# A new order of all five instruction queues in a fused linear-attention and GEGLU block

## The chip, the core and the metric

The kernel runs on one core of a Trainium2 chip. The time is device microseconds of one execution; the figure for a kernel is the median of its runs. A profiled execution, taken by the hardware profiler, stands beside the runs and has a time of its own. The engines are called as in the profile: PE is TensorE, DVE is VectorE, ACT is ScalarE, POOL is GpSimd and SP is SyncE, which here only issues DMAs. POOL issues the stores and some other DMAs.

## The reference

The input x has 2048 rows of 1024 values in bf16. The work is a block with two residual branches, both conditioned by a vector c:

```python
mod = (_silu(c) @ w_mod).reshape(1, 6, 1, -1)
sa, ca, ga, sb, cb, gb = (mod[:, i] for i in range(6))
h = layernorm(x) * (1 + ca) + sa
x = x + ga * A(h, wqkv, wo)          # linear attention, 32 heads of 32
h = layernorm(x) * (1 + cb) + sb
x = x + gb * ((gelu(h @ w_gate) * (h @ w_up)) @ w_down)   # inner width 3584
```

A takes phi(t) = (t + 1 where t > 0, else exp(t)) + 1e-6 of q and k, forms kv = sum of phi(k) v and z = sum of phi(k) per head, and returns (phi(q) kv) / (phi(q) z + 1e-6), multiplied by wo.

## The kernel before, in words

**The work.** Matrix products are done in float16 by schemes of seven products in place of eight, in part nested once more. They need sums and differences of blocks of the operands and of the results; most of these are `tt_op` (L786) on VectorE, and copies out of PSUM on ScalarE (L1092). The rows are handled in two halves of 1024, g = 0 and g = 1. In the profiled execution of before the stages lie about so:

| stage | us from the span's start |
|---|---|
| start: first rows normed, conditioning vector, first weights | 0 to 30 |
| `kvq_phase`: products for k, v and q | 30 to 156 |
| `merge_phase` and `wo_phase`: attention output, first residual, second norm of half 0 | 156 to 240 |
| `gate_up(0)`: gate and up products of half 0 | 240 to 409 |
| `down_out(0)`: down product of half 0 | 409 to 478 |
| `gate_up(1)` | 478 to 650 |
| `down_out(1)` | 650 to 732 |

The places in the code that the prediction speaks of:

- `late_norm(1)` (L1484 to L1503) norms the eight tiles (128 rows each) of half 1 while `gate_up(0)` runs. A tile is loaded into one of three buffers (`x2e_ring`), its statistics are taken on ScalarE (L1494, L1495), completed on VectorE (L1496, L1498) and POOL (L1497, a `pow`), the normed tile is written on ScalarE into one of three buffers (`xhe_ring`, L1499), and POOL stores it to DRAM (L1500). Tiles 0, 3 and 6 use the same buffer of the ring.
- `h2_load` (L1471 to L1474) brings the stored tiles back turned, by a transposing DMA on SP's queue (L1473); `h2_mod` then scales and shifts them. `rows_turned` (L1049) is the same for the first norm.
- `down_out(g)` begins with the differences A1x = A21 − A22 and A11 − A21, in seven steps c of two tiles each (L1921, L1922). A1x lies at 144 KB of a partition, and both rings of `late_norm` lie there too (`x2e_ring` at 144 KB, `xhe_ring` at 150 KB, 2 KB for each buffer), so c = 0 to 2 write over `x2e_ring`, and c = 3, 4, 5 over the three buffers of `xhe_ring`.
- In `down_out`, `nested` (loads L1991, products L2001, 256 wide) and `plain` (loads L1948, products L1952, 512 wide) are the seven products; "b11", "b21", "t0", "t1" and so on name the one. A load goes into memory that an earlier product's weights held.
- In `gate_up`, the products are L1723 (512 wide) and L1734 (256 wide).

**What sets the order.** Nothing is issued as the code is run. Each operation is recorded in a `Plan` with its engine, its predecessors (by memory) and a modelled cost. `Plan.order` then makes a list schedule: it sweeps forward and back over the operations with the modelled costs and due times, keeps the best of 32 forward sweeps, and hands it to `refine`. `refine` moves each engine's operations by a table written into the file: word i of `SHIFTS[engine]` says how many places away the operation stands that is to come at place i ("z13" is thirteen places that keep theirs):

```python
seqs[e] = [seqs[e][i + d] for i, d in enumerate(shifts)]
```

So the table alone decides the final order of each queue. TensorE has 4515 recorded operations, VectorE 1425, ScalarE 815, POOL 191 and SP 233. An engine takes its queue strictly in that order and waits at each operation for the semaphores of its predecessors.

Of the kernel before, what the change touches and what calls it, by code (L numbers as in the profile page):

```python
# [21 lines left out]
        "z13 8 8 8 8 z4 -8 -8 -8 -8 z20 16 16 16 16 -4 -4 -4 -4 -4 -4 -4 -4 -4 -4 -4 -4 -4 -4 -4 -4 4 4 4 4 -4 -4 -4 "  # L22
        "-4 16 16 16 16 -4 -4 -4 -4 -4 -4 -4 -4 z4 4 4 4 4 -12 -12 -12 -12 20 20 20 20 -4 -4 -4 -4 -4 -4 -4 -4 -4 -4 "
        "-4 -4 -4 -4 -4 -4 8 8 8 8 8 8 8 8 8 8 8 8 8 8 8 8 -12 -12 -12 -12 4 4 4 4 4 4 4 4 16 16 16 16 -36 -36 -36 -36 "
        "4 4 4 4 -4 -4 -4 -4 -12 -12 -12 -12 4 4 4 4 -4 -4 -4 -4 4 4 4 4 4 4 4 4 4 4 4 4 4 4 4 4 12 12 12 12 4 4 4 4 "
        "-4 -4 -4 -4 -28 -28 -28 -28 32 32 32 32 32 32 32 32 z8 -16 -16 -16 -16 -16 -16 -16 -16 16 16 16 16 16 16 16 "
        "16 -16 -16 -16 -16 -16 -16 -16 -16 -16 -16 -16 -16 -16 -16 -16 -16 16 16 16 16 16 16 16 16 -8 -8 -8 -8 -8 -8 "
        "-8 -8 -8 -8 -8 -8 -8 -8 -8 -8 z8 16 16 16 16 16 16 16 16 16 16 16 16 -12 -12 -12 -12 -12 -12 -12 -12 -12 -12 "
        "-12 -12 -12 -12 -12 -12 8 8 8 8 8 8 8 8 20 20 20 20 20 20 20 20 28 28 28 28 28 28 28 28 -24 -24 -24 -24 33 33 "
        "33 33 33 33 33 33 -20 -20 -20 -20 -20 -20 -20 -20 -20 -20 -20 -20 -44 -44 -44 -44 34 34 34 34 34 34 34 34 -24 "  # L30
        "-24 -24 -24 -24 -24 -24 -24 -11 -11 -11 -11 -3 -21 -21 -21 -21 -21 32 32 32 32 32 32 32 32 -4 -4 -4 -4 -12 "
        "-12 -12 -12 24 24 24 24 24 24 24 24 -32 -32 -32 -32 -32 -32 -32 -32 -16 -16 -16 -16 -12 -12 -12 -12 -20 -20 "
        "-20 -20 -16 -16 -16 -16 4 4 4 4 40 40 40 40 -8 -8 -8 -8 28 28 28 28 4 4 4 4 36 36 36 36 z4 32 32 32 32 -24 "
        "-24 -24 -24 -24 -24 -24 -24 -24 -24 -24 -24 36 36 36 36 36 36 36 36 -24 -24 -24 -24 -8 -8 -8 -8 -8 -8 -8 -8 "
        "-32 -32 -32 -32 -32 -32 -32 -32 4 4 4 4 -8 -8 -8 -8 -16 -16 -16 -16 32 32 32 32 4 4 4 4 4 4 4 4 -24 -24 -24 "
        "-24 -12 -12 -12 -12 8 8 8 8 24 24 24 24 12 12 12 12 -16 -16 -16 -16 z4 -16 -16 -16 -16 z4 -28 -28 -28 -28 4 4 "
        "4 4 -4 -4 -4 -4 4 4 4 4 -4 -4 -4 -4 4 4 4 4 -4 -4 -4 -4 4 4 4 4 -4 -4 -4 -4 4 4 4 4 -4 -4 -4 -4 z8 36 36 36 "
        "36 z4 4 4 4 4 4 4 4 4 -8 -8 -8 -8 -20 -20 -20 -20 16 16 16 16 -8 -8 -8 -8 -8 -8 -8 -8 -8 -8 -8 -8 -8 -8 -8 -8 "
        "z20 8 8 8 8 -4 -4 -4 -4 -4 -4 -4 -4 24 24 24 24 16 16 16 16 8 8 8 8 z4 -16 -16 -16 -16 -16 -16 -16 -16 -16 "
        "-16 -16 -16 4 4 4 4 -4 -4 -4 -4 4 4 4 4 12 12 12 12 12 12 12 12 -12 -12 -12 -12 -4 -4 -4 -4 16 16 16 16 8 8 8 "  # L40
        "8 -4 -4 -4 -4 8 8 8 8 8 8 8 8 -12 -12 -12 -12 -36 -36 -36 -36 4 4 4 4 -4 -4 -4 -4 z4 64 75 -2 -2 -2 -2 2 2 2 "
        "2 -6 -6 -6 -6 30 62 62 62 62 62 62 62 -6 -6 -6 -6 19 19 19 19 19 19 19 19 19 19 19 -13 -13 -13 -13 -21 -21 "
        "-21 -21 -33 -33 -33 -33 -21 -21 -21 -21 12 12 12 12 12 12 12 12 12 12 -31 -31 -31 -31 8 32 32 32 32 32 32 32 "
        "32 8 8 8 8 8 8 8 8 32 32 32 32 32 32 32 32 32 32 32 32 32 32 32 32 -64 -64 -64 -64 -64 -64 -64 -64 -48 -48 "
        "-48 -48 -56 -56 -56 -56 -20 -20 -20 -20 28 28 28 28 -32 -32 -32 -32 -16 -16 -16 -16 20 -25 -25 -25 -25 3 3 3 "
        "3 -5 -5 -5 -5 8 16 16 16 16 16 16 16 16 16 16 16 16 16 16 16 16 -18 -18 -18 -18 -34 -34 -34 -34 -16 -16 -16 "
        "-16 -16 -16 -16 -16 8 8 -2 -2 -2 -2 -2 -2 -2 -2 4 4 4 4 4 14 12 -7 -7 -7 -7 -1 -1 -1 -1 -6 -2 -2 -2 -2 18 18 "
        "2 2 2 2 -6 -6 -6 -6 4 4 4 4 -4 -4 -4 -4 2 2 2 2 -13 -15 14 5 5 5 5 -5 -5 -5 -5 6 -6 -1 -1 -1 -1 -10 10 10 10 "
        "10 z6 4 4 4 4 -14 -14 -14 -14 z13 35 35 35 35 35 35 35 35 11 11 11 11 11 11 11 11 11 11 11 11 11 11 11 11 27 "
        "27 27 27 27 27 27 27 11 11 11 11 11 11 11 11 -40 -40 -40 -40 -40 -40 -40 -40 -40 -40 -40 -40 -40 -40 -40 -40 "  # L50
        "-40 -40 -40 z8 64 64 64 64 4 4 4 4 4 4 4 4 -12 -12 -12 -12 -12 -12 -12 -12 -4 -4 -4 -4 -4 -4 -4 -4 -4 -4 -4 "
        "-4 -4 -4 -4 -4 -4 -4 -4 -4 -4 -4 -4 -4 -4 -4 -4 -4 -4 -4 -4 -4 -4 -4 -4 -4 -4 -4 -4 -4 -4 -4 -4 -4 -4 -4 -4 "
        "-4 8 8 8 8 8 8 8 8 -8 -8 -8 -8 -8 -8 -8 -8 z8 12 12 12 12 4 4 4 4 -8 -8 -8 -8 -8 -8 -8 -8 z12 20 20 20 20 -4 "
        "-4 -4 -4 16 16 16 16 -8 -8 -8 -8 -8 -8 -8 -8 16 16 16 16 16 16 16 16 -16 -16 -16 -16 -16 -16 -16 -16 16 16 16 "
        "16 4 4 4 4 12 12 12 12 -20 -20 -20 -20 -4 -4 -4 -4 -24 -24 -24 -24 4 4 4 4 -4 -4 -4 -4 2 2 2 2 10 10 10 10 -8 "
        "-3 -3 -3 -3 5 5 5 5 5 5 5 5 -20 -12 -12 -12 -12 4 4 4 4 -4 -4 -4 -4 4 4 4 4 8 8 8 8 12 12 12 12 -12 -12 -12 "
        "-12 -8 -8 -8 -8 12 12 12 12 -8 -8 -8 -8 -4 -4 -4 -4 10 10 6 6 24 24 24 24 -12 -12 -12 -12 -8 -8 -8 -8 4 4 -2 "
        "-2 -2 -2 -10 -10 -10 -10 6 6 6 6 12 12 -6 -6 4 4 4 4 6 6 -18 -18 -18 -18 -8 -8 10 10 10 10 -4 -4 -4 -4 -4 -4 "
        "-4 -4 10 10 10 10 34 34 34 34 -12 -12 -6 -6 -6 -6 6 6 2 2 -16 -16 -6 -6 -6 -6 28 28 4 4 26 26 -8 -8 -8 -8 14 "
        "14 14 14 -30 -30 -4 -4 z4 20 20 20 20 -18 -18 -18 -18 -8 -8 -30 -30 -30 -30 -4 -4 -4 -4 -4 -4 -4 -4 38 38 38 "  # L60
        "38 -8 -8 4 4 4 4 -6 -6 -6 -6 z4 2 2 -2 -2 -20 -20 -16 -16 -4 -4 -4 -4 z2 4 4 -2 -2 -2 -2 14 14 14 14 z4 -20 "
        "-20 -20 -20 -4 -4 -4 -4 -4 -4 50 50 50 50 -4 -4 -4 -4 2 2 2 2 10 10 10 10 -12 -12 -12 -12 10 10 10 10 -16 -16 "
        "40 40 -14 -14 34 34 -16 -16 -16 -16 -10 -10 -10 -10 8 8 z2 -10 -10 -10 -10 -10 -10 -10 -10 8 8 8 8 2 2 -38 "
        "-38 16 16 -8 -8 -8 -8 16 16 z4 -28 -28 -28 -28 -4 -4 -4 -4 -2 -2 -2 -2 6 6 6 6 30 30 30 30 2 2 2 2 4 4 z2 -16 "
        "-16 -16 -16 28 28 28 28 -2 -2 -2 -2 4 4 -26 -26 -6 -6 -16 -16 -16 -16 6 6 6 6 z2 -6 -6 -6 -6 4 4 4 4 -24 -24 "
        "-24 -24 18 18 18 18 -4 -4 -4 -4 -4 -4 18 18 14 14 32 32 32 32 -12 -12 -12 -12 -10 -10 -10 -10 -4 -4 -4 -4 30 "
        "30 -22 -22 -18 -18 2 2 24 24 4 4 -12 -12 -12 -12 4 4 4 4 4 4 4 4 4 4 -16 -16 -16 -16 8 8 8 8 8 8 -2 -2 -2 -2 "
        "-36 -36 -36 -36 12 12 12 12 z2 -6 -6 -6 -6 -4 -4 -4 -4 26 26 4 4 -8 -8 2 2 20 20 z4 10 10 -14 -14 -14 -14 -2 "
        "-2 18 18 18 18 -12 -12 -12 -12 4 4 -12 -12 -12 -12 z4 4 4 4 4 4 4 4 4 18 18 -20 -20 -20 -20 14 14 38 38 38 38 "
        "-6 -6 -6 -6 10 10 10 10 -8 -8 -8 -8 36 36 -4 -4 -4 -4 -20 -20 12 12 -30 -30 -6 -6 -6 -6 -2 -2 12 12 -10 -10 "  # L70
        "-10 -10 14 14 14 14 14 14 24 24 16 16 -42 -42 -10 -10 -10 -10 4 4 4 4 18 18 18 18 -16 -16 -16 -16 18 18 -38 "
        "-38 -38 -38 14 14 -10 -10 -10 -10 -8 -8 -8 -8 22 22 22 22 16 16 8 8 -10 -10 -10 -10 -20 -20 -8 -8 -8 -8 20 20 "
        "10 10 -12 -12 -12 -12 10 10 4 4 4 4 8 8 8 8 -10 -10 -10 -10 -24 -24 -24 -24 4 4 16 16 16 16 -6 -6 -6 -6 18 18 "
        "-2 -2 12 12 -10 -10 -10 -10 26 26 26 26 -12 -12 -12 -12 -12 -12 -8 -8 -8 -8 10 10 24 24 z2 -10 -10 -10 -10 "
        "-10 -10 -10 -10 6 6 z4 8 8 z4 4 4 4 4 10 10 10 10 -28 -28 -28 -28 14 14 14 14 2 2 -6 -6 -12 -12 -12 -12 12 12 "
        "8 8 26 26 26 26 -12 -12 -12 -12 -6 -6 -6 -6 30 30 10 10 2 2 -22 -22 20 20 -12 -12 -12 -12 -12 -12 -12 -12 -10 "
        "-10 -10 -10 2 2 2 2 14 14 -6 -6 -12 -12 -12 -12 2 2 2 2 -6 -6 -6 -6 z4 8 8 8 8 -2 -2 -2 -2 8 8 -4 -4 -12 -12 "
# [2139 lines left out]
```

## Time and profile before

| | us |
|---|---|
| median of 3 runs | 731.52 |
| the runs | 731.52, 739.47, 729.92 |
| profiled execution, its own time | 733.73 |
| its span in the trace | 732.0 |
| PE busy | 719.9 |
| DVE busy | 649.6 |
| ACT busy | 463.2 |
| POOL busy | 134.8 |
| DMA queue q1 (issued by SP and others), share of 16 engines | 57.1% |
| DMA queue q0 (issued by POOL), share of 16 engines | 23.5% |

The span is the time from the first to the last record of the trace; the execution's own time is 1.73 us longer. Busy time leaves out semaphore waits and the issuing of DMAs on SP. The mean granted clock of TensorE over the span was 0.998 of full speed.

### The profile page before, as it was taken

To read this page: it belongs to the slowest core of one execution; us is meant where nothing else is said; L and a number is where in the kernel's file an instruction comes from. 1 tells how busy PE (TensorE), PEld (TensorE's weight loads), DVE (VectorE), ACT (ScalarE), POOL (GpSimd) and SP (SyncE) were. 2 spreads that over 40 slices of the span, in tenths; PEclk is the share of its full clock that TensorE was granted. 3 is DMA by queue.
4 is the path that set the end of the run, shared out by engine and by line. 5 is a ranking of instruction groups with operands and counts; after the bars stand their busy time and mean duration, and the time that the engine had idled before them with its cause. 6 is when DMAs were issued, how large, how long until landed. Compare 5 with 4: busy or idle time off the path is not lost.

```text
span 732.0 us, 12465 instructions
## 1 busy us (share of the span) xinstructions
PE 719.9 (98%) x4504; PEld 417.9 (57%) x4515; DVE 649.6 (89%) x1438; ACT 463.2 (63%) x845; POOL 134.8 (18%) x212
## 2 busy tenths in 40 slices
PE   8999999999999999999989999999999999999997
PEld 4344545444444455555545786755555555568884
DVE  6699998799889999999979997798887998889977
ACT  5584765669787899998867651127777766761220
POOL 2242732011021231523112000121011200000012
PEclk9999999999999999999999999999999999999999
DMA  9977697889999987998898999894337733589995
GB/s 313 320 188 230 151 181 185 315 305 297 285 294 259 292 225 204 267 273 241 238 217 240 239 252 292 262 193 104 100 116 169 176 88 116 151 240 286 260 279 88
DMA packets 183326, 163.42 MB, mean 223 GB/s; under 512 B 34848, under 2 KB 163616, under 8 KB 183264
## 3 DMA queue, kind: packets, MB, share of 16 engines
q1 hardware_dynamic: 156352, 120.93, 57.1%
q0 software_dynamic: 25888, 40.90, 23.5%
q10 hardware_dynamic: 1024, 0.79, 0.3%
q8 instruction: 35, 0.57, 0.3%
q14 instruction: 27, 0.22, 0.1%
HBM read 128.39 MB, written 41.55 MB: 232 GB/s over the span
## 4 chain that ended last, share of the span: by engine, by line
PE 65%; issue 18%; DMA 6%; DVE 6%; ACT 3%; SPq 1%; POOL 1%; ACTq 0%; DVEq 0%; POOLq 0%
PE psum L1723 23%; PE psum L1155 8%; PE psum L1734 8%; PE psum L2001 7%; DVE mem L786 5%; PE psum L1225 5%; PE psum L1254 3%; PE psum L1603 3%; PE psum L1952 3%; DMA mem<-in_A_x_dram 3%; PE psum L1537 2%; DMA out_dram<-mem 1%; DMA xhs<-mem 1%; PE psum L1269 1%; DMA mem<-in_B_w_up_dram 1%
## 5 line engine op out<-in xcount | busy, mean ns | idle before, releaser
L786 DVE TENSOR_TENSOR mem<-mem 128x512 f16<-128x512 f16 (+12 forms) x820 | 371.3, 494 | 9.7 <-DMA out_dram<-mem 1.5
L1723 PE MATMUL psum<-mem 128*128 128x512 f16 x1144 | 275.2, 381 | 2.8 <-DVE mem L786 2.5
L1092 ACT ACTIVATE mem<-psum 128x512 f32<-128x512 f32 (+3 forms) x316 | 164.3, 554 | 106.3 <-PE psum L2001 44.9
L786 DVE TENSOR_TENSOR mem<-psum,mem 128x512 f16<-128x512 f32 (+4 forms) x221 | 164.1, 749 | 26.2 <-PE psum L2001 5.1
L1723 PEld LDWEIGHTS <-mem 128*128 128x128 f16 (+1 forms) x1144 | 112.1, 98 | 107.1 <-issue 5.5
L2001 PE MATMUL psum<-mem 128*128 128x256 f16 (+1 forms) x1078 | 120.1, 273 | 0.0
L2001 PEld LDWEIGHTS <-mem 128*128 128x128 f16 x1078 | 105.5, 98 | 15.3 <-issue 0.2
L1734 PE MATMUL psum<-mem 128*128 128x256 f16 x742 | 105.2, 273 | 0.3 <-DVE psum L786 0.3
L1734 PEld LDWEIGHTS <-mem 128*128 128x128 f16 (+1 forms) x742 | 72.5, 98 | 40.8 <-issue 1.1
L1155 PE MATMUL psum<-mem 128*128 128x512 f16 (+1 forms) x273 | 61.9, 379 | 0.3
L1929 POOL DMA_DIRECT2D out_dram<-mem x14 | 17.1, 1538 | 221.6 <-DVE mem L786 221.6
L786 DVE TENSOR_TENSOR psum<-psum,mem 128x256 f32<-128x256 f32 x106 | 44.1, 425 | 14.8 <-ACT mem L1092 14.3
L1225 PE MATMUL psum<-mem 128*128 128x512 f16 x224 | 51.7, 379 | 0.1
L1780 ACT ACTIVATE psum<-psum 128x512 f32<-128x512 f32 x56 | 32.6, 586 | 28.6 <-PE psum L1734 14.9
L1155 PEld LDWEIGHTS <-mem 128*128 128x128 f16 x280 | 27.0, 98 | 31.8 <-DVE mem L1051 0.5
L1952 PE MATMUL psum<-mem 128*128 128x512 f16 (+2 forms) x196 | 37.8, 349 | 0.0
L1799 ACT ACTIVATE mem<-psum 128x512 f16<-128x512 f32 x56 | 32.7, 596 | 7.1 <-PE psum L1723 7.0
L1225 PEld LDWEIGHTS <-mem 128*128 128x128 f16 (+1 forms) x224 | 21.4, 98 | 25.5 <-issue 1.1
L1809 ACT ACTIVATE mem<-mem 128x512 f16<-128x512 f16 x56 | 34.9, 632 | 0.5 <-DVE mem L786 0.5
L1254 PE MATMUL psum<-mem 128*128 128x512 bf16 x124 | 28.6, 379 | 0.9 <-DVE mem L1027 0.5
L1537 PE MATMUL psum<-mem 128*128 128x512 f16 x128 | 28.4, 379 | 0.1
L1952 PEld LDWEIGHTS <-mem 128*128 128x128 f16 x196 | 18.1, 98 | 16.8
(149 smaller groups left out, 631.5 us busy)
## 6 DMA issues: line engine op xcount, KB each, us to landing
mem<-in_B_w_gate_dram SPq DMA_DIRECT2D x14, 1024.0 KB, 5.8
mem<-in_B_w_up_dram SPq DMA_DIRECT2D x14, 1024.0 KB, 5.4
mem<-in_w_mod_dram SPq DMA_DIRECT2D x24, 512.0 KB, 6.6
mem<-us SPq DMA_DIRECT2D x24, 448.0 KB, 6.8
mem<-vs SPq DMA_DIRECT2D x20, 448.0 KB, 6.7
mem<-in_B_w_down_dram SPq DMA_DIRECT2D x18, 448.0 KB, 7.0
ts<-in_B_w_down_dram POOLq DMA_DIRECT2D x28, 256.0 KB, 5.5
mem<-ts SPq DMA_DIRECT2D x15, 448.0 KB, 7.3
```

The costliest lines, as they stand in the source:

```text
L786: ve.tensor_tensor(out=out, in0=a, in1=b, op=op)
L1092: ac.activation(out=t, in_=ps, func=AF.Copy)
L1155: te.matmul(ps, lhsT=A[:, k, i * P:(i + 1) * P], rhs=B[:, k, :], start=(start and k == 0), stop=(k == KH - 1), skip_group_check=True)
L1225: te.matmul(o, lhsT=W[:, k, (j0 + i) * P:(j0 + i + 1) * P], rhs=h_form(a, k), start=(start and k == 0), stop=(k == KH - 1), skip_group_che ...
L1254: te.matmul(ps, lhsT=hr1[b][:, k, tl * P:(tl + 1) * P], rhs=Wk[:, k, n * NW:(n + 1) * NW], start=(k == 0), stop=(k == KD - 1))
L1537: te.matmul(psw[:, half, :], lhsT=pqT[b][:, g, tl * P:(tl + 1) * P], rhs=Wp[:, g, half * NW:(half + 1) * NW], start=(g == 0), stop=(g == K ...
L1723: te.matmul(ps, lhsT=a[:, k, e, :], rhs=b[:, k, :], start=(start and k == 0), stop=(k == KH - 1), skip_group_check=True)
L1734: te.matmul(ps, lhsT=self.x[a][:, k, :], rhs=self.y[y][:, k, :], start=(start and k == 0), stop=(k == KH // 2 - 1), skip_group_check=True)
L1799: ac.activation(out=o, in_=ps, func=AF.Gelu_apprx_tanh)
L1809: ac.activation(out=o, in_=o, func=AF.Gelu_apprx_tanh)
L1952: te.matmul(psm[:, b, c], lhsT=A[:, i, q * P:(q + 1) * P], rhs=wt[:, i, c], start=(start and i == 0), stop=(i == NPR - 1), skip_group_chec ...
L2001: te.matmul(ps[:, q, :], lhsT=a[:, k, q * P:(q + 1) * P], rhs=y[:, k, :], start=(start and q == 0 and k == 0), stop=(k == NPR // 2 - 1), s ...
```

## The change

The tables of all five engines in `SHIFTS` are replaced (L19 to L206). Nothing else in the file differs: the same operations with the same tiles, shapes and predecessors are issued by the same engines, in another order. The new tables come from a plan that counts longer latencies for the late stores of normed tiles and for blocks that a DMA turns. The diff has 350 lines of such numbers; here is POOL's table in part:

```diff
     "POOL": (
...
-        "7 15 15 10 7 10 8 5 11 1 -1 10 12 10 11 12 10 1 -59 11 -51 10 -33 13 5 17 -38 -36 5 -36 4 8 5 5 -40 14 11 -42 "
-        "-10 15 z1 4 14 -23 -1 -23 -11 -3 -2 10 10 -19 1 -2 -13 -5 1 -5 5 2 -12 4 z1 4 4 4 z1 -3 2 5 -15 z1 1 -1 -16 "
...
+        "16 10 7 12 10 3 4 5 9 -2 9 11 9 10 11 9 -27 -60 10 15 7 -35 -55 17 5 -5 12 5 7 2 -43 -13 4 -42 9 2 -43 10 3 6 "
+        "12 -49 12 -17 z1 13 -16 8 -15 -7 -1 -12 -4 8 -8 8 -5 z1 1 -9 5 6 4 -3 z1 -3 2 3 -15 -13 2 z1 -3 z1 3 z1 -2 2 "
```

Read as places in the queues (counted from 0), the old tables against the new ones give this:

| engine | operations that change place | longest move | of these, in the prediction |
|---|---|---|---|
| PE | 2368 of 4515 | 56 | one group of 14 products of "b21" in `down_out(0)` goes behind 14 others |
| DVE | 1233 of 1425 | 93 | L1921 of `down_out(0)`: c = 0 from 750 to 768, c = 1 from 827 to 814, c = 3 from 765 to 829, the others by at most 9; L1496 of tile 6 from 691 to 701; some sums of weight halves in `gate_up` earlier |
| ACT | 516 of 815 | 29 | L1499 of tile 6 from 409 to 410; the first `h2_mod` behind the second L1473 of half 1's second block from 506 to 524 |
| POOL | 146 of 191 | 18 | L1500 of tile 0 from 125 to 113, tile 1 from 126 to 121, tile 2 from 137 to 143, tile 3 from 134 to 144; L1497 of tile 5 from 143 to 140 and of tile 6 from 146 to 142 |
| SP | 141 of 233 | 11 | the last transposing load of `h2_load` (L1473) from 141 to 146, behind five loads of `down_out(0)` |

344 rows, old and new, of the table SHIFTS are left out of this document.

## The prediction

> **What bounds the kernel now.** I read the head of the page, then the waits of TensorE, then the chain of waits around the one long wait, then the windows of the stages.
>
> ```profile
> span 732.0 us, 12465 instructions
> PE 719.9 (98%) x4504; PEld 417.9 (57%) x4515; DVE 649.6 (89%) x1438; ACT 463.2 (63%) x845; POOL 134.8 (18%) x212
> ```
>
> TensorE is the bound: it is busy for all but 12.1 us of the span (732.0 − 719.9), and the change removes none of its instructions. A new order can only win those 12.1 us, and whatever part of the 719.9 us was run at a low clock. The waits of TensorE that another engine ended (columns: total, times, longest, us):
>
> ```profile
> PE psum L1723 <- DVE mem L786: 2.5, 1, 2.5
> PE psum L900 <- POOL mem masks.py:199: 1.5, 1, 1.5
> PE psum L1269 <- DVE mem L786: 0.6, 1, 0.6
> PE psum L907 <- DVE mem L893: 0.6, 1, 0.6
> PE psum L1254 <- DVE mem L1027: 0.5, 1, 0.5
> PE psum L907 <- ACT mem L909: 0.5, 1, 0.5
> PE psum L1734 <- DVE psum L786: 0.3, 1, 0.3
> PE psum L1254 <- ACT mem L924: 0.2, 1, 0.2
> ```
>
> Their sum is 6.7 us. Only the first is long. 2% of 731.52 us, about what a measurement of this kernel can tell from no change, is 14.6 us, more than twice the sum. The chain of waits shows what made the long one (columns: start, duration, what):
>
> ```profile
> 361.81 0.53 POOL xhs L1500
> 362.34 8.96 DMA xhs<-mem
> 371.31 0.02 issue
> 371.33 0.07 DVE mem L1921
> 371.40 0.54 issue
> 371.94 1.57 DVE mem L786 x4
> 373.51 0.04 issue
> 373.55 3.56 PE psum L1723 x8
> ```
>
> The store of the normed tile 6 of `late_norm` (L1500) leaves from an `xhe_ring` slot. `down_out`'s L1921 writes A1x over the same memory, so it must wait until the store has landed, 8.96 us after its issue. L1921 stands in VectorE's queue ahead of four sums (L786) that TensorE needs. The wait costs more than itself, as TensorE's timeline and the windows show (columns of the windows: window, length, PE, PEld, DVE, ACT, POOL busy with counts, granted clock, DMA share, GB/s):
>
> ```profile
> 373.55 3.56 PE L1723 MATMUL psum<-mem 128*128 128x512 f16 x8 [2.55 <-DVE mem L786]
> 377.39 3.63 PE L1723 MATMUL psum<-mem 128*128 128x512 f16 x16
> ...
> 356.00:370.80 14.80, 14.80 (x88) 8.43 (x86) 11.77 (x31) 13.14 (x28) 3.83 (x7) 1.00 1.04 268
> 370.80:373.50 2.70, 0.20 (x1) 0.00 (x0) 2.17 (x6) 0.95 (x3) 0.82 (x1) 1.00 0.92 296
> 373.50:376.80 3.30, 3.25 (x8) 1.17 (x8) 3.23 (x10) 0.00 (x0) 0.00 (x0) 0.51 1.21 252
> ```
>
> The eight matmuls behind the wait took 3.56 us, while sixteen of the same shape took 3.63 us right after: eight cost 1.82 us at full clock, so 1.74 us more went to a granted clock of 0.51. [...]
>
> **The change, part by part.** Only the table of places changes, for all five queues; every operation, tile and byte stays. So the terms are waits removed and waits made.
>
> (1) *The waiting L1921 (the one of c = 3).* It goes from place 765 of VectorE's queue to 829. A place is worth 649.6 us / 1438 = 0.45 us of work, or 732.0 / 1438 = 0.51 us of span; 64 places are 29 to 33 us. It then runs near 400 us, some 29 us after the store landed at 371.3. The four sums come up at about 370 us and TensorE finds them done. Removed: 2.55 us of wait and 1.74 us of low clock, **−4.3 us**. What is late next? The other L1921 operations keep places from 768 to 841, behind the landing as well, and L1921 itself is only read in `down_out`, from about 409 us on; nothing new stands behind it. The bounds of this term: −4.3 us, and −2.55 us if the low clock does not come from the wait.
>
> (2) *Stores of normed tiles on POOL.* Those of tiles 0 and 1 go 12 and 5 places earlier, those of tiles 2 and 3 go later, behind the `pow` (L1497) of tiles 5 and 6.
>
> ```profile
> 318.42 0.54 POOL L1500 DMA_DIRECT2D xhs<-mem  x1
> 321.09 1.30 POOL L1500 DMA_DIRECT2D xhs<-mem  x1
> 337.94 0.67 POOL L1497 TENSOR_TENSOR mem<-mem 128x1 f32<-128x1 f32 x1 [3.98 <-DVE mem L1496]
> 339.96 1.69 POOL L1497 TENSOR_TENSOR mem<-mem 128x1 f32<-128x1 f32 x1
> 352.33 1.23 ACT L1499 ACTIVATE mem<-mem 128x1024 f16<-128x1024 bf16 x1
> DMA to landing us min/median/max: 3.2/6.9/9.1
> ```
>
> The last row is that of L1500's stores. The `pow` waits for VectorE's L1496, and tile 6's L1496 goes 10 places later, 10 × 0.51 = 5.1 us: the `pow` that began at 339.96 begins near 345.1 and ends 0.67 to 1.69 us later, and tile 3's store goes second behind it (0.54 us each): issued at 346.3 to 347.3 instead of near 321. It lands 3.2, 6.9 or 9.1 us later: at 349.5 at the earliest, near 353.7 by the median, at 356.4 at the latest. ScalarE's L1499 of tile 6 (352.33) writes tile 3's `xhe_ring` slot, as the ring has three; it stands in ScalarE's queue ahead of evictions that TensorE's banks wait for. So ScalarE waits 0, 1.4 or 4.1 us. ScalarE had 14.80 − 13.14 = 1.7 us free in the next 14.8 us, but not all ahead of the first eviction. I charge TensorE half of the median wait, **+0.7 us**; bounds 0 and 4.1 us, with the low clock behind the latter.
>
> (3) *Loads of `down_out(0)` behind the turned block.* The second transposing load (L1473) goes behind five loads of SP's queue, and a group of fourteen 256-wide matmuls of b21 (L2001) goes behind fourteen others.
>
> ```profile
> 401.38 6.35 SPq L1473 DMA_TRANSPOSE mem<-xhs  x1
> 430.58 1.91 SPq L1948 DMA_DIRECT2D mem<-ts  x2
> DMA to landing us min/median/max: 7.0/7.2/7.3
> 426.79 11.55 PE L2001 MATMUL psum<-mem 128*128 128x256 f16 x103
> 438.17 6.21 PE L1952 MATMUL psum<-mem 128*128 128x512 f16 x28
> ```
>
> The transpose holds SP's queue for 6.35 us; the five loads that now go ahead of it gain up to that, and its first reader, an `h2_mod` on ScalarE, goes 18 places later as well: nothing lost there. [...] The fourteen moved matmuls cost 14 × 11.55 / 103 = 1.57 us, and they free the memory into which the second half of "t1" is loaded (L1948). That load was issued by 430.58 + 1.91 = 432.49 at the latest, landed 7.0 us after (the third row, of L1948), at 439.5 at the latest, and is first used after seven of the twenty-eight L1952 matmuls: 438.17 + 7 × 6.21 / 28 = 439.72. There is a margin of at least 0.2 us; issued 1.57 us later, the load comes 1.0 to 1.4 us late: **+1.0 us**; bounds 0 (the matmuls that went ahead also end earlier) and 1.4 us, or 3.1 us with the low clock behind it.
>
> (4) *Everything else.* 2368 of TensorE's 4515 places and 1233 of VectorE's 1425 recorded places change, by up to 56 and 93. Some sums of the weight halves in `gate_up` come 3 to 5 us earlier on VectorE, close to the landing of their loads.
>
> ```profile
> 240.00:360.00 120.00, 119.57 (x687) 66.85 (x686) 116.64 (x309) 107.74 (x220) 35.06 (x48) 1.00 0.86 249
> 409.00:478.00 69.00, 69.00 (x552) 53.91 (x551) 59.92 (x99) 23.12 (x39) 4.99 (x4) 1.00 0.98 265
> 478.00:560.00 82.00, 82.00 (x470) 45.80 (x469) 69.50 (x170) 52.13 (x110) 11.39 (x14) 1.00 0.55 132
> ```
>
> From 240 to 360 us VectorE is busy 116.64 of 120 us and TensorE 119.57: a wait of VectorE there has 3.4 us to vanish in, no more. From 478 us on VectorE has 12.5 us free in 82, and such waits vanish. Gain bound: the small waits of 0.2 to 0.6 us (2.7 us together; the 1.5 us is the start's mask and stays). Those at L907 sit in the start behind the loads, so their removal is mostly lost. Loss bound: the 3 us of VectorE's earlier takings plus some waits of 0.3 us. I take **+0.8 us**, near the short waits seen before, since every chain's spacing stays as tight as it was.
>
> Sum: 733.73 (the profiled execution's own time; 1.73 us around its span of 732.0) − 4.3 + 0.7 + 1.0 + 0.8 = 731.9. That execution lay 2.2 us over the median of the runs (733.73 − 731.52); with that taken off, **729.8 us**, 0.2% under before.
>
> **The rivals.**
>
> *Full gain.* Neither (2) nor (3) nor (4) makes a wait: 733.73 − 4.3 − 2.2 = 727.2 us. For it: the store may land in 3.2 us. Against it: (3) has a margin of some tenths against a delay of 1.57 us.
>
> *A late store takes the place of the late L1921* (the other side). The store of tile 3 takes the longest landing, the 8.96 or 9.1 us that tile 6's took. ScalarE's L1499 waits 4.1 us, TensorE runs out of banks, and its clock falls again: 4.1 + 1.7 = 5.8 instead of 0.7. 733.73 − 4.3 + 5.8 + 1.0 + 0.8 − 2.2 = 734.8 us, slower than before. It decides from the point where this stall passes 4.3 − 1.0 − 0.8 = 2.5 us. For it: a DMA share of 1.04 in the window from 356 on, when the long landing was seen. Against it: the share is 0.86 over the stage from 240 us, and tiles 2 and 3 store when half of them land in 6.9 us.
>
> *The gain is given back in `down_out(0)`.* DMA is at 0.98 of the 16 engines there, so each load waits its turn. If the loads moved by the transpose make a second late load beside "t1" (3.1 us with the clock), the sum is 733.73 − 4.3 + 0.7 + 3.1 + 0.8 − 2.2 = 731.8 us: no change.
>
> *The low clock stays.* By the row with 0.51, it may be that the clock falls for a cause other than the wait, or falls at another gap. Then (1) is worth 2.55 us: 731.5 us. [...]
>
> *The tight chains break.* With half of TensorE's places moved, waits of 0.2 to 0.6 us like those of the list could come at many places. To be slower by 2% they must add 14.6 + 4.3 = 18.9 us, more than all 12.1 us of today's idle time: some 47 waits of 0.4 us. As a middle, fifteen of them: 733.73 − 4.3 + 6.0 + 0.7 + 1.0 − 2.2 = 734.9 us.
>
> **How the numbers follow.** Forecast 0.40, full gain 0.13, late store 0.17, given back 0.12, low clock stays 0.05, tight chains 0.13. The low end: all small waits that can go gone as well, 727.2 − 1.7 = 725.5. The high end: both upper bounds together, late store 5.8 and load 3.1, and 3 us of (4): 733.73 − 4.3 + 5.8 + 3.1 + 3.0 − 2.2 = 739.1. For the forecast alone 728 to 732. Cases that gain something hold 0.58 to 0.7, yet none of them reaches 2%: faster by over 2% needs all waits gone and more, 0.02. Slower by over 2% comes from the tight chains' upper part alone, 0.07. Within 2%: 0.91.
>
> **What would show it.** Right: in the list of TensorE's waits the 2.5 us of L1723 behind L786 is gone, L1921 does not follow a store's landing, the clock is 1.00 in all windows from 356 to 409; POOL's stores of tiles 2 and 3 near 346 us; a wait of about 1 us at L1952 near 440 us. Wrong: a new wait above 2 us anywhere on TensorE, above all behind L1499 near 353 us; a fall of the clock in another window; a TensorE busy time far from 718 us; or many new waits behind L786 or L1092 from 240 to 360 us.

## The result, and the profile after

The changed kernel took 730.65 us in the median of 20 runs (729.09 to 733.74); the kernel before, now with 20 runs, 734.64 us (729.92 to 739.56). The ratio is 0.9956, 95% interval 0.9935 to 0.9977: faster by 0.44% (the two medians alone give 0.9946). The interval reaches 0.2% to each side, so it tells far smaller changes than the 2% that the prediction took. The forecast of 729.8 us and its range hold; the profiled execution went from 733.73 to 730.54 us, by 3.2 us where the sum of the prediction said 1.8.

The head of the page and TensorE's waits of the changed kernel (columns: total, times, longest):

```profile
span 728.7 us, 12496 instructions
PE 719.5 (99%) x4515; PEld 417.8 (57%) x4515; DVE 649.3 (89%) x1438; ACT 464.3 (64%) x845; POOL 135.6 (19%) x212
```

```profile
PE psum L900 <- POOL mem masks.py:199: 1.5, 1, 1.5
PE psum L1734 <- DVE psum L786: 1.2, 1, 1.2
PE psum L1254 <- DVE mem L1027: 0.8, 1, 0.8
PE psum L1269 <- DVE mem L786: 0.8, 1, 0.8
PE psum L921 <- DVE mem L913: 0.4, 1, 0.4
PE psum L1254 <- ACT mem L1261: 0.2, 1, 0.2
PE psum L1155 <- ACT mem L1092: 0.2, 1, 0.2
PE psum L907 <- DVE mem L893: 0.2, 1, 0.2
```

The 2.5 us of L1723 is gone; the largest rise is that of L1734, from 0.3 to 1.2 us. The sum is 5.3 us instead of 6.7. The windows of the stretch where the long wait was:

```profile
356.00:370.80 14.80, 14.80 (x91) 8.58 (x88) 14.49 (x40) 12.85 (x26) 2.42 (x5) 1.00 1.03 233
370.80:376.80 6.00, 6.00 (x34) 3.23 (x33) 5.40 (x14) 4.28 (x10) 1.80 (x3) 1.00 1.08 310
376.80:409.00 32.20, 32.20 (x194) 18.72 (x192) 30.27 (x71) 24.80 (x50) 5.13 (x6) 1.00 1.03 243
```

TensorE is busy throughout and at full clock. So of the 3.3 us that the span lost (732.0 − 728.7), 6.7 − 5.3 = 1.4 us are waits and some 1.7 us the low clock that came behind the long one; 0.2 us remain.

Two POOL timelines, before and then after, show something that the prediction had not seen (columns: start, duration; in brackets the idle time ahead and what ended it):

```profile
361.81 1.07 POOL L1500 DMA_DIRECT2D xhs<-mem  x2 [7.99 <-ACT mem L1499]
```

```profile
346.40 1.67 POOL L1500 DMA_DIRECT2D xhs<-mem  x3
...
355.71 0.54 POOL L1500 DMA_DIRECT2D xhs<-mem  x1 [0.75 <-ACT mem L1092]
363.87 0.54 POOL L1500 DMA_DIRECT2D xhs<-mem  x1 [7.62 <-ACT mem L1092]
```

Before, POOL stood idle for 8 us until tile 5 was written, then sent the stores of tile 5 and tile 6 one right behind the other. Tile 6 had been written first, by ScalarE from 352.33 to 353.56 us. The new order puts tile 6's store (place 150 to 148) ahead of tile 5's: it goes out at 355.71 us instead of 362.34.

### The profile page after: what moved, and what is told of

It reads as the page before. It is cut to its first block, busy times and chain, and to the rows that moved or that the text cites. A ratio compares the mean times of both kernels' runs of the same rounds, so it can differ in the third digit from the quotient of the medians.

```text
span 728.7 us, 12496 instructions
## 1 busy us (share of the span) xinstructions
PE 719.5 (99%) x4515; PEld 417.8 (57%) x4515; DVE 649.3 (89%) x1438; ACT 464.3 (64%) x845; POOL 135.6 (19%) x212
## 4 chain that ended last, share of the span: by engine, by line
PE 85%; DVE 4%; DMA 3%; ACT 2%; POOL 2%; issue 2%; SPq 1%; POOLq 0%; DVEq 0%; ACTq 0%
PE psum L1723 31%; PE psum L2001 16%; PE psum L1734 10%; PE psum L1225 7%; PE psum L1155 6%; PE psum L1952 5%; PE psum L1537 4%; PE psum L1603 3%; DVE mem L786 3%; DMA mem<-in_A_x_dram 2%; PE psum L1254 1%; DMA mem<-ts 1%; SPq L831 1%; PE psum L1269 1%; ACT mem L1063 1%
## 5 line engine op out<-in xcount | busy, mean ns | idle before, releaser
L786 DVE TENSOR_TENSOR mem<-mem 128x512 f16<-128x512 f16 (+13 forms) x820 | 372.9, 494 | 12.9 <-DMA mem<-ts 1.5
L1723 PE MATMUL psum<-mem 128*128 128x512 f16 x1144 | 273.6, 379 | 0.1
L786 DVE TENSOR_TENSOR mem<-psum,mem 128x512 f16<-128x512 f32 (+5 forms) x221 | 164.0, 750 | 28.2 <-PE psum L1734 6.0
L1723 PEld LDWEIGHTS <-mem 128*128 128x128 f16 (+1 forms) x1144 | 111.8, 98 | 102.4 <-issue 0.4
L2001 PEld LDWEIGHTS <-mem 128*128 128x128 f16 x1078 | 105.4, 98 | 14.9 <-DVE mem L786 0.2
L1734 PE MATMUL psum<-mem 128*128 128x256 f16 x742 | 105.8, 273 | 1.2 <-DVE psum L786 1.2
L1734 PEld LDWEIGHTS <-mem 128*128 128x128 f16 (+1 forms) x742 | 72.5, 98 | 42.3 <-issue 1.8
L786 DVE TENSOR_TENSOR psum<-psum,mem 128x256 f32<-128x256 f32 x106 | 44.6, 426 | 11.4 <-ACT mem L1092 11.1
L1155 PEld LDWEIGHTS <-mem 128*128 128x128 f16 x280 | 27.1, 98 | 32.0 <-issue 0.5
L1952 PE MATMUL psum<-mem 128*128 128x512 f16 (+2 forms) x196 | 37.8, 349 | 0.0
L1333 POOL DMA_DIRECT2D ts<-in_B_w_down_dram x28 | 27.5, 1259 | 7.0 <-DMA ts<-in_B_w_down_dram 6.6
```

The source lines that it names most:

```text
L786: ve.tensor_tensor(out=out, in0=a, in1=b, op=op)
L1155: te.matmul(ps, lhsT=A[:, k, i * P:(i + 1) * P], rhs=B[:, k, :], start=(start and k == 0), stop=(k == KH - 1), skip_group_check=True)
L1723: te.matmul(ps, lhsT=a[:, k, e, :], rhs=b[:, k, :], start=(start and k == 0), stop=(k == KH - 1), skip_group_check=True)
L1734: te.matmul(ps, lhsT=self.x[a][:, k, :], rhs=self.y[y][:, k, :], start=(start and k == 0), stop=(k == KH // 2 - 1), skip_group_check=True)
L1952: te.matmul(psm[:, b, c], lhsT=A[:, i, q * P:(q + 1) * P], rhs=wt[:, i, c], start=(start and i == 0), stop=(i == NPR - 1), skip_group_chec ...
L2001: te.matmul(ps[:, q, :], lhsT=a[:, k, q * P:(q + 1) * P], rhs=y[:, k, :], start=(start and q == 0 and k == 0), stop=(k == NPR // 2 - 1), s ...
```

## The experiments

The experiments move single operations in one of the two orders. Each adds two lines to `refine`, behind the line that applies the table, so that L1921 reads L1923 in their profiles, L1500 reads L1502, L786 reads L788, and so on:

```diff
             seqs[e] = [seqs[e][i + d] for i, d in enumerate(shifts)]
+        for e, a, b in [('DVE', 765, 829)]:
+            seqs[e].insert(b, seqs[e].pop(a))
```

**One move in the old order.** The edit is the one above.

> The kernel before with one operation moved: VectorE's L1921 of c = 3 from place 765 to 829, everything else in the old order. Theory W (the wait at this one operation, with the low clock behind it, is the gain of the whole change): the 2.5 us wait of PE's L1723 is gone, no low clock after 370 us, own time 733.7 - 4.3 = 729.4 us, ratio to before 0.992 to 0.996, as good as or a little better than the whole change (0.9956), since the new waits of the new order (1.2 us near 303 us, 0.7 us near 45 us) are not there; and the runs lie within some 5 us of each other instead of 10, if it is the landing of the store that makes the runs of before differ. Rival S (the gain is spread over the new order): less than half of it, ratio 0.998 or more. Rival N (the spread of before comes from elsewhere): the runs keep a spread near 10 us.

Median 730.75 us (12 runs, 729.44 to 734.57), ratio 0.9953 (0.9929 to 0.9977); span 728.2 us. No wait of L1723 is left and the clock stays up:

```profile
368.00:376.00 8.00, 8.00 (x46) 4.29 (x44) 7.60 (x20) 6.33 (x12) 2.24 (x3) 1.00 1.01 289
```

One of some 4400 moves does as much as all of them. The span fell by 3.8 us, not by the 4.3 expected, because the other waits of its profile add up to 4.7 us instead of 4.2. Theory W holds, S falls. The 12 runs lie within 5.1 us, those of before beside them within 9.0, so N falls as well.

**The same operation back, in the new order.**

```diff
+        for e, a, b in [('DVE', 829, 766)]:
```

> The changed kernel with L1921 of c = 3 put back ahead of the sums that were behind it before (VectorE place 829 to 766), everything else in the new order. Theory W: L1921 stands there near 369.5 us and waits for tile 6's store, which landed at 373.6 us in the profile of after; PE waits 2 to 4 us and runs 1.7 us slower behind it, so 4 to 6 us come back: own time 734.5 to 736.5 us, ratio to before 0.998 to 1.004, runs spread over 10 us again. Rival S: it costs under 2 us, ratio 0.995 to 0.998, because other operations of the new order carry the gain.

Median 731.07 us, ratio 0.9954 (0.9928 to 0.998). Theory W missed: nothing came back. The ratio is in the range of rival S, and so is the reason, as another operation of the new order carries the gain too:

```profile
370.80 0.68 DVE L1923 TENSOR_TENSOR mem<-mem 128x1024 f16<-128x1024 f16 x1
```

L1921 runs at 370.80 us with no idle time ahead of it, because tile 6's store had gone out at 355.30 us and landed at 359.99. The new order removes the wait twice: by moving the one that waits, and by sending what it waits for earlier. In the profile of after, the store that landed at 373.6 us was tile 5's, not tile 6's as the expectation had it.

**The other remedy alone, in the old order.**

```diff
+        for e, a, b in [('POOL', 150, 149)]:
```

> The kernel before with one exchange on POOL: tile 6's store (L1500, place 150) ahead of tile 5's (149), L1921 left at its old place 765. In the profile of before tile 6 was written on ScalarE from 352.33 us on, but its store went out at 362.34 only, behind tile 5's, whose tile was written 8 us later. Theory Q (the store was late because of what stood ahead of it in POOL's queue): it goes out near 354 us, lands before 364 us, L1921 does not wait at 368, and the whole gain is there without moving L1921: ratio 0.993 to 0.997, no wait of PE's L1723. Rival L (the long landing of 9 us belongs to the DMA load of that stretch and comes with any place): the store lands at 363 us or later, but still ahead of 368: no wait either; then only a landing above 14 us would bring one. Rival W2 (only the place of L1921 counts): the ratio stays at 1.000.

Median 731.74 us (729.78 to 733.75), ratio 0.9955 (0.9926 to 0.9984):

```profile
355.88 0.54 POOL L1502 DMA_DIRECT2D xhs<-mem  x1
363.60 0.54 POOL L1502 DMA_DIRECT2D xhs<-mem  x1 [7.17 <-ACT mem L1501]
```

Tile 6's store goes out at 355.88 and landed 6.6 us later, at 362.5; L1921 does not wait. The gain is there without any move on VectorE. Theory Q holds: the store was late because of its place in POOL's queue.

**Both remedies taken out of the new order.**

```diff
+        for e, a, b in [('DVE', 829, 766), ('POOL', 148, 149)]:
```

> The changed kernel with both taken back: L1921 of c = 3 from place 829 to 766 on VectorE, and tile 6's store behind tile 5's on POOL (148 and 149 exchanged). Moving L1921 back alone had cost nothing, as the new order also sends tile 6's store earlier (355.71 instead of 362.34 us). Theory Q+W (either of the two is enough, both gone bring the wait back): the store goes out near 364.4 us, lands near 373.5, L1921 waits from 369.5 on, PE waits 2.5 to 4 us and loses 1 to 1.7 us to the clock: own time 734 to 736 us, ratio 0.998 to 1.003. Rival: the new order has other cover (more sums done ahead), PE waits under 1.5 us: ratio up to 0.997.

Median 731.88 us (730.25 to 736.48), ratio 0.9954 (0.9927 to 0.9982).

```profile
369.91 0.69 DVE L1923 TENSOR_TENSOR mem<-mem 128x1024 f16<-128x1024 f16 x1 [0.99 <-DMA xhs<-mem]
```

```profile
371.00 0.60 PE L1736 MATMUL psum<-mem 128*128 128x256 f16 x4 [1.53 <-DVE psum L788]
```

L1923 waits for the store again, but TensorE waits only 1.53 us: the store went out at 363.48 and landed 6.4 us later, not the 9 us on which the expectation rested. In e2_move_back, where L1921 does not wait, the same products waited 0.44 us, so about 1.1 of the 1.53 us are the store's. The clock stayed at 1.00. By the ratio this is the rival's range (up to 0.997); the median does not return to that of before. Three of the twelve runs, 734.91, 735.03 and 736.48 us, are as long as theory Q+W expected, two of them with a mean granted clock of 0.997. That fits a longer landing in those executions, but they were not profiled.

Why the landings near 363 us are mostly shorter in this order is not settled. The traces hold a trail. In all six profiles with the old order of SP's queue, the transposing load (L1473 of the kernel before) that SP issued at 359 to 361 us was still under way when the store went out. It took 11.8, 13.1, 13.8, 14.4, 15.4 and 16.2 us to land (e1_one_move, before, e4_before_again, e5_store_swap, e10_two_moves, e7_earlier), and the later of the stores issued from 361 us on took 7.9, 9.0, 9.6, 10.6, 12.1 and 12.2 us, in the same order, and landed about 1 us ahead of it each time. In the profiles of the new order the landing of that load is not in the trace. No run moves that load, so this shows that the two go together, not which of them holds up the other.

**The kernel before, profiled again.**

> The kernel before, profiled a second time. If the landing of tile 6's store sets the wait and varies between executions, this profile shows another length of the wait at L1921 and PE's L1723 and a span that differs from 732.0 us by as much, with the low clock after it again. If the wait is fixed by the order alone, it is 2.5 us again to some tenths.

Its time was 734.44 us, span 732.7.

```profile
371.90 0.69 DVE L1921 TENSOR_TENSOR mem<-mem 128x1024 f16<-128x1024 f16 x1 [4.02 <-DMA xhs<-mem]
```

```profile
374.12 2.58 PE L1723 MATMUL psum<-mem 128*128 128x512 f16 x8 [3.18 <-DVE mem L786]
376.49 1.06 PE L1734 MATMUL psum<-mem 128*128 128x256 f16 x4
377.34 4.23 PE L1723 MATMUL psum<-mem 128*128 128x512 f16 x16
```

The same store landed 0.6 us later after its issue (9.6 instead of 9.0 us) and the wait is longer by 0.6 us. So in these two profiles the order fixes where the wait is and the landing how long it is.

This fits the spread of the kernel before, though the runs of that spread were not profiled. Of 35 runs, the 16 with a mean granted clock of 0.999 or 1.0 have a median of 732.3 us and the 19 with 0.998 or less one of 737.2 us. The changed kernel's 20 runs show 0.999 or 1.0 in all but its longest one.

**A longer wait.** The old order, L1921 eight places earlier.

```diff
+        for e, a, b in [('DVE', 765, 757)]:
```

> The kernel before with L1921 of c = 3 eight places earlier (765 to 757), so that VectorE stands still from about 365 us until the store lands near 371.5, with the sums that PE needs at 368.2 behind it. Theory C (the low clock is a fixed price of a wait above some 2.5 us): PE waits 5 to 7 us, in one or two pieces, and loses 1.3 to 1.7 us to the clock as before: ratio 1.004 to 1.006. Rival P (the stretch of low clock grows with the wait): 3 us or more at the low clock's price, ratio 1.006 to 1.009. Rival R (sums caught up on hide the longer wait): ratio 1.000 to 1.003.

Median 739.47 us (732.84 to 741.89) against 735.10, 0.6% more; the ratio with its interval is 1.0033 (1.0002 to 1.0065).

```profile
377.39 1.86 PE L1736 MATMUL psum<-mem 128*128 128x256 f16 x8 [8.54 <-DVE psum L788]
379.05 5.09 PE L1725 MATMUL psum<-mem 128*128 128x512 f16 x16
```

```profile
371.80:377.39 5.59, 0.00 (x0) 0.00 (x0) 2.34 (x7) 0.36 (x1) 0.00 (x0) 0.50 0.42 118
377.30:380.00 2.70, 2.61 (x11) 1.52 (x11) 2.70 (x9) 2.67 (x5) 1.43 (x3) 0.50 0.12 47
380.00:383.00 3.00, 3.00 (x11) 1.13 (x10) 1.93 (x7) 1.05 (x3) 0.81 (x1) 0.66 0.54 88
383.00:386.00 3.00, 3.00 (x18) 1.52 (x17) 2.68 (x5) 1.33 (x3) 0.00 (x0) 1.00 1.29 246
```

TensorE waited 8.54 us (the store landed 12.2 us after its issue) and lost 2.70 × 0.50 + 3.00 × 0.34 = 2.4 us to the clock. A wait more than three times as long lost 2.4 us instead of 1.7. Neither theory fits as written: C said 1.3 to 1.7 us for a wait of 5 to 7, P 3 us or more. The stretch of low clock did grow with the wait, as P has it: it ran from 371.8 to 382.0 us. But 5.6 of these 10.2 us lie in the wait itself (first row), where TensorE has no product to slow down.

**Tile 3's store still later, in the new order.**

```diff
+        for e, a, b in [('POOL', 144, 147)]:
```

> The changed kernel with tile 3's store (L1500, POOL place 144) three places later, behind a store that went out at 354.42 us. Tile 6 is written into the same buffer by ScalarE (L1499, 354.18 us), which then waits for a landing near 358.5 to 362. This is the prediction's rival of the late store at a known size. Theory F (ScalarE's wait goes on to PE in full): ScalarE waits 4 to 8 us, PE as long, and the clock falls: ratio 1.001 to 1.008. Theory H (half of it is hidden by what PE has ahead): PE waits 2 to 4 us, ratio 0.998 to 1.003. Rival A (absorbed, as ScalarE has free time): ratio as the changed kernel, 0.9955.

Median 737.56 us (736.51 to 742.37), ratio 1.0038 (1.0006 to 1.0069): slower than before.

```profile
359.64 1.24 ACT L1501 ACTIVATE mem<-mem 128x1024 f16<-128x1024 bf16 x1 [5.71 <-DMA xhs<-mem]
```

```profile
361.69 3.57 PE L1725 MATMUL psum<-mem 128*128 128x512 f16 x8 [5.14 <-ACT mem L1094]
```

```profile
361.60:365.00 3.40, 3.31 (x8) 1.17 (x8) 3.34 (x10) 2.53 (x6) 0.12 (x1) 0.50 0.35 105
365.00:368.00 3.00, 3.00 (x18) 1.80 (x17) 1.83 (x5) 2.28 (x6) 0.00 (x0) 0.91 0.45 151
```

ScalarE waited 5.71 us and TensorE 5.14, nine tenths of it, and lost 3.40 × 0.50 + 3.00 × 0.09 = 2.0 us more. Theory F holds: what the late-store rival described did happen here. In the profile of the changed kernel tile 3's store had landed near 350.6 us, 3.6 us ahead of L1499.

**The one new wait of the changed kernel.** In its profile VectorE waited for a load of weights:

```profile
300.63 1.42 DVE L786 TENSOR_TENSOR mem<-mem 128x1024 f16<-128x1024 f16 x2 [1.51 <-DMA mem<-ts]
```

```profile
303.16 0.38 PE L1734 MATMUL psum<-mem 128*128 128x256 f16 x2 [1.18 <-DVE psum L786]
```

```diff
+        for e, a, b in [('DVE', 581, 591), ('DVE', 581, 591)]:
```

> The changed kernel with two sums of a weight block (L786 on VectorE, places 581 and 582, the first readers of an L1369 load that landed at 300.5 us) put ten places later. Theory: PE's wait of 1.18 us for L1734 near 303 us is VectorE's wait for that load and is gone: own time 730.5 - 1.2 = 729.3 us, ratio to before 0.994. Rival: the load's landing of 6.4 us (2.7 us in the profile of before) is a chance of that execution, or the time goes into the next wait; then the median stays that of the changed kernel, ratio 0.9955 or more.

Median 730.62 us, ratio 0.9951 (0.9926 to 0.9976). The wait near 303 us is gone from the profile. The ratio lies between the 0.994 of the theory and the 0.9955 of the rival, and the interval holds both: 1.2 us are 0.16%, too little for the time to decide. The other profiles with the changed kernel's order untouched at that place speak for the rival: e2_move_back has 0.29 us there, e9_group_later 0.46, e6_both_back and e8_store_later none. Most of the 1.18 us belonged to that execution.

**The load of t1's weights.** The changed kernel has no wait at L1952, where the prediction put 1.0 us. The move stands seven times in the list:

```diff
+        for e, a, b in [('PE', 2512, 2532)] * 7:
```

> The changed kernel with the last seven products of b21's group (L2001, PE places 2512 to 2518) put behind the fourteen that follow, so that the memory for the second half of t1's weights (L1948) comes free 14 x 0.11 = 1.5 us later still, near 432.9 instead of 431.4 us, while L1952 needs them near 437.3 as before. Theory M (the predicted wait was missing because the load landed in 4.4 us, the other half's, instead of 7.0): it lands at 437.3 to 439, PE waits 0 to 2 us at L1952 (0 at 4.4 us, 1.5 at 5.9 us). Rival: another path frees or hides it, then no wait of L1952 whatever the landing, or the moved products make PE wait somewhere else near 432 to 436 us.

One run, 730.15 us. The products of t1, first in the changed kernel and then here:

```profile
428.28 3.43 SPq L1948 DMA_DIRECT2D mem<-ts  x2
```

```profile
435.73 6.21 PE L1952 MATMUL psum<-mem 128*128 128x512 f16 x28
```

```profile
427.74 4.96 SPq L1950 DMA_DIRECT2D mem<-ts  x2
```

```profile
435.19 6.33 PE L1954 MATMUL psum<-mem 128*128 128x512 f16 x28
```

The second half was issued by 428.28 + 3.43 = 431.7 us, and here by 432.7; its first use is at 435.73 + 7 × 6.21 / 28 = 437.3, and here at 436.8. The 28 products took 0.12 us more here, the most that can be wait. So the load landed within some 4.5 us of its issue, which is what theory M gives at its edge; as the landing itself is not in the trace, that it was hidden in another way is not ruled out. The first halves landed after 4.4 us in both.

**Both remedies alone, in the old order.**

```diff
+        for e, a, b in [('DVE', 765, 829), ('POOL', 150, 149)]:
```

> The kernel before with only the two moves that each sufficed alone: L1921 of c = 3 from 765 to 829 on VectorE, and tile 6's store ahead of tile 5's on POOL; all else in the old order. If these two hold the whole gain, it equals the changed kernel: median 730 to 731 us, ratio 0.994 to 0.996, runs within 5 us, no wait of PE over 1 us after 60 us. If the rest of the new order carries something of its own, it stays 1 us or more above the changed kernel's 730.65.

Median 730.38 us (729.56 to 732.66), ratio 0.9961 (0.9936 to 0.9985), span 728.2 us; no wait of TensorE over 0.6 us behind the start's 1.5. Two moves equal the whole table, within the intervals. No kernel here beats the changed one clearly.

## Why the prediction was right or wrong

**The bound and the main term (1) were right.** The wait and the low clock, 2.55 + 1.74 us, went as forecast with −4.3. e1_one_move shows that this one operation is enough.

**Its cause was only half seen.** The prediction took tile 6's store as fixed, landing at 371.3 us, and read its 8.96 us as the length of a DMA. Behind it stood POOL's queue: the store was held from 353.6 to 362.3 us by another tile's. The places of tile 6's store, 150 to 148, were in the same table, and the prediction listed tiles 0 to 3 alone. e5_store_swap shows that this exchange would have been enough too.

**Term (2) was mis-sized, and its share to TensorE too.** Tile 3's store was forecast at 346.3 to 347.3 us and went out at 347.0, second of three. (Before, it had gone out at 318.42 us, not near 321: the row at 321.09 is tile 2's, by their places 134 and 137. The sum does not use it.) The landing was the wrong part. The first row is that of all L1500 stores of the changed kernel, the second of the three from 346.40 us on:

```profile
DMA to landing us min/median/max: 3.1/4.2/9.7
DMA to landing us min/median/max: 3.1/3.6/3.9
```

The median is 4.2 us instead of the 6.9 taken from before, and the three landed by 351.4 us, ahead of ScalarE's L1499 (354.18 us). So 0 us instead of 0.7. And in e8_store_later, where ScalarE did wait, nine tenths went on to TensorE (5.14 of 5.71 us), not the half that was charged. The rival's price, all of ScalarE's 4.1 us and 1.7 us of low clock, was the better estimate: e8_store_later has 5.14 + 2.0 us for a wait of 5.71.

**Term (3) was mis-sized in the same way.** The later issue was right: from the issue to the first use there were 439.72 − 432.49 = 7.2 us, and now 437.3 − 431.7 = 5.6. The 7.0 us that the prediction took were this load's own landing in the profile of before. Here it must have landed within about 5.6 us, as TensorE did not wait; the row of all L1948 loads of the changed kernel shows how far such landings lie apart:

```profile
DMA to landing us min/median/max: 4.4/5.9/10.5
```

So 0 us instead of 1.0. Both times a landing of one execution was taken as that of the place.

**Term (4), +0.8 us,** was about right: the small waits went from 4.2 us (6.7 − 2.5) to 5.3. Part of that is luck, as the 1.2 us near 303 us are 0 to 0.5 us in the four other profiles with the same order there.

**The step from the profiled execution to the median failed.** The prediction took off 2.2 us, because three runs had a median of 731.52. With 20 runs it is 734.64, 0.9 us above the profiled execution. The 20 runs of this kernel, whose wait hangs on a landing, spread over 9.6 us (729.92 to 739.56), and three of them said little of its median. The forecast number came close by luck: the changed kernel's median lies 0.1 us above its profiled execution, not 2.2 below, and this error of 2.3 us was partly cancelled by the 1.7 us of waits that did not come. The forecast fall of the median was 1.7 us, the measured one 4.0.

**The rivals.** The full gain (no new wait from terms 2 to 4) comes nearest in the profiled execution, with −4.3 us where −3.2 was measured and the forecast's sum had −1.8. The late store was not reached. "The low clock stays" fell: the windows from 356 to 409 us are all at 1.00.

## What to carry to other kernels

When an instruction waits for a store's landing, look at the store's own queue before its DMA: here a store stood behind another tile's for 8.8 us, about as long as its own landing took (8.96 us), and the remedy was at either end of the wait. Before a wide spread between runs is put down to the chip, look for a wait on a transfer with a margin near zero. In this kernel the TensorE waits of 2.55, 3.18, 5.14 and 8.54 us cost their length plus 1.7 to 2.4 us of low clock; those of 1.18 and 1.53 us came with a granted clock of 1.00 and cost their length alone, and no profile has a wait in between. Three runs are too few for the median of a kernel that spreads over 10 us.

## What the runs showed of the hardware

The granted clock fell with TensorE waits of 2.55, 3.18, 5.14 and 8.54 us, to 0.51 in the row of the first and 0.50 in those of the last two (windows that reach beyond the low stretch of the second have 0.72 from 374.1 and 0.58 from 376.5 us). It was 1.00 behind waits of 1.18 and 1.53 us:

```profile
371.00:374.00 3.00, 3.00 (x18) 1.76 (x18) 2.75 (x7) 1.85 (x5) 0.00 (x0) 1.00 0.33 108
```

This row is e6_both_back, right behind its 1.53 us. The lengths that follow are estimates from the granted clocks of the windows, with the low clock taken as half. The stretch of low clock was 3.4 us long with the two shorter waits, 6.8 us with the third (358.7 to 365.5 us of e8_store_later) and 10.2 us with the fourth (371.8 to 382.0 us of e7_earlier). With the two longer ones it began in the wait itself, 2.2 and 2.9 us after its start; in e4_before_again it began 1.0 us after the wait had ended. Only the part behind the wait cost time, 3.4, 3.4, 3.8 and 4.6 us of it at half speed; in the part inside it TensorE had nothing to do (0.00 us busy from 371.80 to 377.39 us of e7_earlier). So the price was 1.7 to 2.4 us, not much more for a long wait than for a short one.

The stores of tiles 5 and 6, 256 KB each and issued by POOL between 361.8 and 364.1 us, took 8.9 and 9.0 us to land in the kernel before, and one of them 9.7 us in the changed one, 6.4 in e6_both_back and 12.2 in e7_earlier; tile 2's, issued near 346 us in the changed kernel, took 3.1 us.
